# The low parts of the sums' blocks made by a multiplication and an accumulating DMA, in a channel attention kernel with a squared-relu feed-forward

## The chip, the cores and the metric

The kernel runs on one core of a Trainium2 chip. The metric is the device time of that core in microseconds. The engines have short names in the profile: PE is TensorE (PEld its weight loads), ACT is ScalarE, DVE is VectorE, POOL is GpSimd, SP is SyncE. SP issues all of the kernel's DMAs before the change.

## The reference

Four batches of 6080 tokens with 256 channels go through an attention over channels, and the 24320 resulting tokens through a feed-forward layer of width 2048 with the square of a relu. All data are float32; the two weight matrices come as float64.

```python
def _attn_ref(q, k, v, tau) -> np.ndarray:
    qn = q / (np.linalg.norm(q, axis=1, keepdims=True) + 1e-06)
    kn = k / (np.linalg.norm(k, axis=1, keepdims=True) + 1e-06)
    s = kn.transpose(0, 2, 1) @ qn / tau
    s = s - s.max(-1, keepdims=True)
    a = np.exp(s)
    a /= a.sum(-1, keepdims=True) + 1e-09
    return (v @ a).astype(np.float32)

def _moe_ref(x, w_in, w_out) -> np.ndarray:
    h = np.maximum(x @ w_in, 0.0)
    return (h * h @ w_out).astype(np.float32)
```

## The kernel before

**What is multiplied.** Attention and the first weight matrix are folded: for each batch the 256x256 attention matrix is multiplied with w_in once (tiles w_hi and w_lo), and the tokens of v then go through that product. So the main loop does two products for each block of tokens: v times the folded matrix (psum tile ps_h), and the squared relu times w_out (psum tile ps_o). For float32 accuracy each operand is split into a high part, rounded to fp32r, and a low part, which is the rest; three of the four products of parts are computed (hi hi, hi lo, lo hi).

**Tiles and steps.** A batch's tokens are cut into 12 blocks: ten of 512 and two of 480 tokens. A block has 16 steps, one for each 128 of the 2048 hidden channels. Two steps make a pair r. Each pair has one tile x of eight slots, each slot half a block wide (256 or 240 elements in a partition), and tiles g_hi and g_lo. `first_product` of a step (lines 712 to 727) does six matmuls into ps_h and one relu on ACT, which writes two of the slots 0 to 3 of x: the even step slots 0 and 1, the odd step slots 2 and 3. After the odd step `squares_and_sums` (736) squares slots 0 to 3 in place.

**Seven products instead of eight.** For all blocks but the first two, and but the last three pairs of the last block (`by_seven`, 704), the second product uses Winograd's scheme on 2x2 blocks: seven products instead of eight. It needs four sums of the squares' blocks, which VectorE writes into slots 4 to 7 of x with three instructions (743 to 746). g_hi and g_lo have seven slots: slots 0 to 2 take the parts of the squares' blocks, x slots 1 to 3 (cast on ACT, 744, and a subtraction of 768 elements on VectorE, 747); slots 3 to 6 take the parts of the four sums, x slots 4 to 7, in `parts_of_sums` (749): a cast of 1024 elements on ACT, and a subtraction of 1024 elements on VectorE. There are 365 such pairs: 46 blocks of eight, less three. Pairs without the scheme have one cast and one subtraction of 1024 elements for slots 0 to 3, in the same function.

**The order of a pair.** The main loop (964 to 1015) numbers the steps i. Every engine executes its instructions in the order in which the program issues them (`InProgramOrder`, 19). With p a pair whose steps are 2p and 2p + 1, the order around it is this:

- i = 2p: `first_product`; the first relu into x of p.
- i = 2p + 1: `first_product`; second relu; `squares_and_sums` of p (square, three sums, parts of slots 0 to 2).
- i = 2p + 2: `first_product` of the next pair; one piece of the attention for a later batch; `parts_of_sums` of p; second product of p - 1, part 0.
- i = 2p + 4: `first_product`, whose relu opens pair p + 2; second product of p, part 0, which reads slots 0, 1 and 2.
- i = 2p + 5: second product of p, part 1, which reads slots 3 to 6, the parts of the sums.

The pieces of attention stand between: for each chunk of q and k (tile qk, two in flight) a cast qk_hi on ACT, a subtraction qk_lo on VectorE, then a square on ACT, an addition into acc on VectorE, and the matmuls into gram (`attention`, 433). At a block's end come two copies of ps_o on ACT and five additions on VectorE (`combine`, 822), then four stores; and the casts of the next block of v (687, 696).

**Buffers.** Tiles of `pool` (96) have two buffers unless told otherwise; x, g_hi and g_lo have two. So pair p + 2 takes the buffers of pair p. ps_h has three (98).

Of the kernel before, what the change touches and what calls it, by code (L numbers as in the profile page):

```python
# [8 lines left out]
F32 = mybir.dt.float32  # L9
# [5 lines left out]
ALU = mybir.AluOpType  # L15
# [15 lines left out]
def kernel(  # L31
# [22 lines left out]
    tensor, vector, scalar, pool_engine = (  # L54
        InProgramOrder(tc, e) for e in (nc.tensor, nc.vector, nc.scalar, nc.gpsimd)
    )
# [647 lines left out]
    def by_seven(b, n, r):  # L704


        return (0, 1) < (b, n) and ((b, n) != order[-1] or r < SWITCH)
# [41 lines left out]
    def parts_of_sums(b, n, r):  # L749

        x = X.pop((b, n, r))
        hi, lo = G[b, n, r]
        if by_seven(b, n, r):
            hi, lo, src = hi[:, 3:7, :], lo[:, 3:7, :], x[:, 4:8, :]
        else:
            src = x[:, 0:4, :]
        scalar.copy(hi, src)
        vector.tensor_sub(lo, src, hi.bitcast(F32))

    O = {}  # L760

# [202 lines left out]
    for i in range(len(steps) + 2 * LAG):  # L964
# [24 lines left out]
        if part == 0 and 0 <= i // 2 - 1 < len(pairs):  # L989
            parts_of_sums(*pairs[i // 2 - 1])  # L990
# [52 lines left out]
```

## Time and profile before

| | us |
|---|---|
| median of the runs shown | 2214.74 |
| the two runs | 2213.72 and 2215.77 |
| span of the profiled execution, first to last instruction | 2211.6 |
| from the profiled span to the median | 3.1 |

The profile is of one execution. It gives, for each engine, the time in which it had an instruction running, and for each group of instructions the mean time of one and the idle time of its engine before it, with what ended most of that. A group's row names engine, operation, the tile written, the tiles read, and the shape (partitions by elements). A row of the timeline begins with the start and the duration in microseconds; what stands in square brackets is the engine's idle time before it and what ended that. A row of waits gives who waited for whom: the sum in microseconds, how many times, and the longest. A row of the DMA list gives size and median time from issue to landing. Line L27 is the helper through which engine instructions are issued, so instructions are told apart by their tiles. Matmuls are pipelined and their ends are modelled, so PE's busy share is not a share of its peak.

### The profile page before, as it was taken

What the parts mean: (1) busy time and instruction counts of PE and PEld (TensorE: products, weight loads), DVE (VectorE), ACT (ScalarE), POOL (GpSimd) and SP (SyncE); (2) the same over time, 40 slices, a digit from 0 to 9 for tenths busy, and PEclk for the clock granted to TensorE, in tenths of its full rate; (3) what the DMA queues carried; (4) which work ended last, traced back from release to release, by engine and by line L of the source; (5) the groups of instructions that cost most, each with busy time, mean ns of one, the idle gap of its engine ahead of it and who ended that gap; (6) DMA issues with size and microseconds to landing.
All of it is one profiled execution on the core that took longest, in us unless ns stands there. A gap on an engine that the chain in (4) does not pass through costs nothing.

```text
span 2211.6 us, 34981 instructions
## 1 busy us (share of the span) xinstructions
PE 2203.1 (100%) x13903; PEld 1985.0 (90%) x13903; DVE 1818.0 (82%) x2614; ACT 1859.1 (84%) x2347; POOL 0.7 (0%) x6
## 2 busy tenths in 40 slices
PE   9999999999999999999999999999999999999999
PEld 8789999988999999998999999999899988888898
DVE  6878888889888888878888888887888877787776
ACT  5788888888888888888878888888888888888887
POOL 0000000000000000000000000000000000000000
PEclk9999999999999999999999999999999999999999
DMA  9521122023421122210122122111103010010000
GB/s 342 179 77 39 61 77 65 27 76 109 157 86 58 60 62 71 63 60 21 36 95 86 60 66 76 58 53 60 33 24 115 22 36 20 22 37 20 20 28 19
DMA packets 82261, 148.03 MB, mean 67 GB/s; under 512 B 8368, under 2 KB 35760, under 8 KB 82096
## 3 DMA queue, kind: packets, MB, share of 16 engines
q1 hardware_dynamic: 82096, 145.79, 19.9%
q8 instruction: 109, 1.79, 0.3%
q14 instruction: 56, 0.46, 0.1%
HBM read 112.46 MB, written 33.29 MB: 66 GB/s over the span
## 4 chain that ended last, share of the span: by engine, by line
PE 92%; DVE 3%; DMA 2%; ACT 2%; issue 0%; SPq 0%; DVEq 0%; ACTq 0%
PE ps_h L27 46%; PE ps_o L27 41%; PE gram L27 4%; PE ps_w L27 2%; DMA qk<-in_k 1%; DVE g_lo L27 1%; DVE x L27 1%; ACT x L27 1%; DMA qk<-in_q 0%; DMA qk_heads<-in_q 0%; ACT g_hi L27 0%; DVE o L27 0%; DMA w_raw<-in_w_in 0%; DVE dec_m L27 0%; DMA wi_lo<-wi_kept 0%
## 5 line engine op out<-in xcount | busy, mean ns | idle before, releaser
L27 DVE TENSOR_TENSOR g_lo<-x,g_hi 128x768 fp32r<-128x768 f32 (+2 forms) x749 | 808.2, 1079 | 71.7 <-ACT g_hi L27 71.1
L27 DVE TENSOR_TENSOR x<-x 128x512 f32<-128x512 f32 (+1 forms) x1095 | 558.2, 510 | 244.0 <-ACT x L27 218.3
L27 ACT CAST g_hi<-x 128x768 fp32r<-128x768 f32 (+2 forms) x749 | 702.1, 937 | 42.8 <-DVE x L27 30.0
L27 ACT ACTIVATE x<-ps_h 128x512 f32<-128x512 f32 (+1 forms) x768 | 456.0, 594 | 248.7 <-PE ps_h L27 228.0
L27 PE MATMUL ps_h<-v_hi,w_hi 128*128 128x512 f32 (+1 forms) x1536 | 478.6, 393 | 0.0
L27 PE MATMUL ps_h<-v_hi,w_lo 128*128 128x512 f32 (+1 forms) x1536 | 477.9, 392 | 0.0
L27 PE MATMUL ps_h<-v_lo,w_hi 128*128 128x512 f32 (+1 forms) x1536 | 474.9, 390 | 0.0
L27 ACT ACTIVATE x<-x 128x1024 f32<-128x1024 f32 (+1 forms) x384 | 404.5, 1053 | 11.9
L27 PE MATMUL ps_o<-g_lo,wS_hi 128*128 128x256 f32 (+1 forms) x1460 | 407.6, 279 | 1.2 <-DVE g_lo L27 1.1
L27 PE MATMUL ps_o<-g_hi,wS_hi 128*128 128x256 f32 (+1 forms) x1460 | 406.1, 278 | 0.8 <-ACT o L27 0.8
L27 PE MATMUL ps_o<-g_hi,wS_lo 128*128 128x256 f32 (+1 forms) x1460 | 406.6, 278 | 0.0
L27 PEld LDWEIGHTS ps_h<-v_lo,w_hi 128*128 128x128 f32 x1536 | 287.9, 187 | 64.9
L27 PEld LDWEIGHTS ps_h<-v_hi,w_lo 128*128 128x128 f32 x1536 | 288.5, 188 | 62.4 <-DVE w_lo L27 0.3
L27 PE MATMUL ps_o<-g_hi,wo_hi 128*128 128x256 f32 (+2 forms) x1159 | 325.2, 285 | 0.6 <-ACT g_hi L27 0.6
L27 PE MATMUL ps_o<-g_hi,wo_lo 128*128 128x256 f32 (+2 forms) x1159 | 325.1, 285 | 0.0
L27 PE MATMUL ps_o<-g_lo,wo_hi 128*128 128x256 f32 (+2 forms) x1159 | 324.8, 285 | 0.1
L27 PEld LDWEIGHTS ps_o<-g_lo,wS_hi 128*128 128x128 f32 x1460 | 274.8, 188 | 17.9 <-DVE g_lo L27 2.1
L27 PEld LDWEIGHTS ps_o<-g_hi,wS_hi 128*128 128x128 f32 x1460 | 274.1, 188 | 17.2 <-ACT o L27 1.6
L27 PEld LDWEIGHTS ps_o<-g_hi,wS_lo 128*128 128x128 f32 x1460 | 274.4, 188 | 0.0
L27 PEld LDWEIGHTS ps_h<-v_hi,w_hi 128*128 128x128 f32 x1536 | 237.4, 188 | 3.6
L27 PEld LDWEIGHTS ps_o<-g_hi,wo_hi 128*128 128x128 f32 x1159 | 218.3, 188 | 15.7 <-ACT g_hi L27 1.0
L27 PEld LDWEIGHTS ps_o<-g_lo,wo_hi 128*128 128x128 f32 x1159 | 217.7, 188 | 15.2 <-DVE g_lo L27 0.5
(120 smaller groups left out, 1776.1 us busy)
## 6 DMA issues: line engine op xcount, KB each, us to landing
qk<-in_k SPq DMA_DIRECT2D x87, 256.0 KB, 2.8
qk<-in_q SPq DMA_DIRECT2D x87, 256.0 KB, 3.0
v<-in_vT SPq DMA_DIRECT2D x40, 512.0 KB, 3.8
out_T<-o SPq DMA_DIRECT2D x152, 128.0 KB, 1.7
wiS<-wi_sums_kept SPq DMA_DIRECT2D x24, 512.0 KB, 5.7
wi_hi<-wi_kept SPq DMA_DIRECT2D x16, 512.0 KB, 4.5
wi_lo<-wi_kept SPq DMA_DIRECT2D x16, 512.0 KB, 3.8
w_raw<-in_w_in SPq DMA_DIRECT2D x4, 1024.0 KB, 6.4
```

Source lines behind the costliest of these rows:

```text
L27: return lambda *args, **kwargs: self.tc.keep_in_program_order(issue(*args, **kwargs))
```

## The change

Only `parts_of_sums` changes, and in it only the pairs with seven products. ACT's cast of the four sums into g_hi stays as it was. VectorE no longer subtracts g_hi from the sums. It multiplies the sums by -1 and writes the result into the low part's four slots, rounded to fp32r: minus the rounded sums. Then POOL issues a DMA that adds the sums (x slots 4 to 7, 4 KB in each partition in a full block) to what stands in g_lo, which leaves the sums less their rounded value. The DMA waits for the multiplication; VectorE's instruction no longer needs g_hi. The other pairs do what they did before.

```diff
@@ -751,11 +751,12 @@
         x = X.pop((b, n, r))
         hi, lo = G[b, n, r]
         if by_seven(b, n, r):
-            hi, lo, src = hi[:, 3:7, :], lo[:, 3:7, :], x[:, 4:8, :]
+            scalar.copy(hi[:, 3:7, :], x[:, 4:8, :])
+            vector.tensor_scalar_mul(lo[:, 3:7, :], x[:, 4:8, :], -1.0)
+            pool_engine.dma_start(lo[:, 3:7, :].bitcast(F32), x[:, 4:8, :], accum_op=ALU.add)
         else:
-            src = x[:, 0:4, :]
-        scalar.copy(hi, src)
-        vector.tensor_sub(lo, src, hi.bitcast(F32))
+            scalar.copy(hi, x[:, 0:4, :])
+            vector.tensor_sub(lo, x[:, 0:4, :], hi.bitcast(F32))
 
     O = {}
```

## The prediction

> **What bounds the kernel now.** I read the page first, then the groups by shape, the waits, the timeline in two stretches, and the list of DMAs.
>
> ```profile
> span 2211.6 us, 34981 instructions
> PE 2203.1 (100%) x13903; PEld 1985.0 (90%) x13903; DVE 1818.0 (82%) x2614; ACT 1859.1 (84%) x2347; POOL 0.7 (0%) x6
> PE 92%; DVE 3%; DMA 2%; ACT 2%; issue 0%; SPq 0%; DVEq 0%; ACTq 0%
> q1 hardware_dynamic: 82096, 145.79, 19.9%
> L27 PEld LDWEIGHTS ps_o<-g_lo,wS_hi x1460: 186/188/193, 169.9 to 2196.4; 128*128 128x128 f32 x183
> ```
>
> PE has work in 2203.1 of 2211.6 us and holds 92% of the chain that ended last. A shorter VectorE instruction can win only the 8.5 us in which PE is without work. The question is what else the change delays. Four matmuls per pair read g_lo against wS_hi (three of them in the part that reads the sums), so the last row counts 1460/4 = 365 pairs with seven products, the first at 169.9 us.
>
> ```profile
> L27 DVE TENSOR_TENSOR g_lo<-x,g_hi 128x1024 fp32r<-128x1024 f32 x320 | 390.5, 1220 | 54.7 <-ACT g_hi L27 54.2
> L27 ACT ACTIVATE x<-ps_h 128x512 f32<-128x512 f32 x640 | 382.8, 598 | 211.3 <-PE ps_h L27 195.9 <-DVE g_lo L27 7.5 <-DVE v_lo L27 1.8
> L27 DVE TENSOR_TENSOR qk_lo<-qk,qk_hi 128x1024 fp32r<-128x1024 f32 x63 | 77.1, 1223 | 26.7 <-ACT qk_hi L27 26.7
> L27 DVE TENSOR_TENSOR acc<-acc,qk 128x1024 f32<-128x1024 f32 x63 | 76.9, 1221 | 12.2 <-ACT qk L27 12.2
> L27 DVE TENSOR_SCALAR dec_e<-w_raw 128x1024 int32<-128x1024 int32 x8 | 5.5, 688 | 0.4 <-DMA w_raw<-in_w_in 0.4
> ACT x L27 <- DVE g_lo L27: 11.6, 15, 1.5
> ...
> 1424.79 1.22 DVE L27 TENSOR_TENSOR g_lo<-x,g_hi 128x1024 fp32r<-128x1024 f32 x1
> 1426.10 0.60 ACT L27 ACTIVATE x<-ps_h 128x512 f32<-128x512 f32 x1 [0.62 <-DVE g_lo L27]
> ```
>
> The last three rows carry the argument. The relu (ACT, `x<-ps_h`) waits for g_lo 15 times, and in the instance shown it starts 0.09 us after the 1024-wide subtraction ends. That subtraction reads slots 4 to 7 of an x tile, and the relu of the pair two later writes slots 0 and 1 of the tile that takes its buffer (x has two). They share no byte, yet the relu waits: the buffer passes on as a whole, when its last reader is done. That reader is what the change replaces.
>
> **The change, part by part.** (1) The cast into g_hi on ACT reads and writes the same 1024 elements as before: nothing.
>
> (2) On 365 pairs the VectorE subtraction (1.22 us) becomes a multiplication by -1 with one tensor operand. No row shows one from f32 to fp32r. The nearest are TENSOR_SCALAR on 1024 elements, 0.69 us, and TENSOR_TENSOR, 1.22 us; I take 0.69, the row with one tensor operand, and keep 1.22 for the range. The 0.53 us saved and the 54.2 us of waiting for g_hi are VectorE's; with PE covering VectorE they are worth nothing by themselves.
>
> (3) A DMA of 512 KB a pair (480 KB in the short blocks) goes out on POOL's queue, empty until now (0.7 us busy), so nothing queues behind it there and SP's queue is not touched. It waits for the multiplication and reads x and g_lo. Its time L, from the end of the multiplication to the landing, is shown by no row. Nearest:
>
> ```profile
> v<-in_vT SPq DMA_DIRECT2D x40, 512.0 KB, 3.8
> w_raw<-in_w_in SPq DMA_DIRECT2D x4, 1024.0 KB, 6.4
> wi_kept<-wi_hi SPq DMA_DIRECT2D x4, 512.0 KB, 2.6
> out_T<-o SPq DMA_DIRECT2D x152, 128.0 KB, 1.7
> 1499.70 0.60 SPq L326 DMA_DIRECT2D qk<-in_q  x1
> ```
>
> An addition in flight reads two operands of 512 KB each and writes one. If only the 512 KB written counted, L would be 2.6 us (a store) to 3.8 us (a load). If the 1024 KB read count, a load of that size took 6.4 us. Between 3.8 and 6.4 I take the middle, 5.1 us: both ends in on-chip memory argue for less, descriptors made by POOL for more. Upper end for the range: 6.4 plus 0.6 (SP's own issue of a DMA), 7.0.
>
> The Trainium skill, "DMA: Bandwidth & Descriptors", section "Anatomy of one DMA — SWDGE (gpsimd) path", gives such a DMA about 2.0 us plus its bytes over 436 GB/s, 3.2 us for 512 KB. Its page "Collectives: The Full Stack", section "The bandwidth ceiling: the fold count and why AG ≠ RS ≠ AR", says that an add in the DMA needs two reads on the same ring; with 1024 KB the first formula gives 4.4 us. By the sum below these are about 2320 and 2565 us. No row of this trace holds an accumulating DMA.
>
> (4) What waits for the landing. First PE: the sums' low part is read in the step five after the pair's first. Second, and earlier, the relu that opens the pair two later, by the hand-over shown above. Behind that relu, in order, stands all of ACT's work: the cast or square of a q/k chunk, the 1024-wide cast of the pair in between, the next relu and square.
>
> ```profile
> 1752.56 0.60 ACT L27 ACTIVATE x<-ps_h 128x512 f32<-128x512 f32 x1 [0.23 <-PE ps_h L27]
> 1753.02 0.95 DVE L27 TENSOR_TENSOR g_lo<-x,g_hi 128x768 fp32r<-128x768 f32 x1
> 1753.13 1.05 ACT L27 CAST g_hi<-x 128x1024 fp32r<-128x1024 f32 x1
> 1754.22 1.22 DVE L27 TENSOR_TENSOR g_lo<-x,g_hi 128x1024 fp32r<-128x1024 f32 x1 [0.25 <-ACT g_hi L27]
> 1758.36 0.60 ACT L27 ACTIVATE x<-ps_h 128x512 f32<-128x512 f32 x1
> 1760.23 0.60 ACT L27 ACTIVATE x<-ps_h 128x512 f32<-128x512 f32 x1 [0.33 <-PE ps_h L27]
> 1760.86 1.06 ACT L27 ACTIVATE x<-x 128x1024 f32<-128x1024 f32 x1
> 1761.95 1.61 DVE L27 TENSOR_TENSOR x<-x 128x512 f32<-128x512 f32 x3 [0.80 <-ACT x L27]
> ...
> 752.28 0.60 ACT L27 ACTIVATE x<-ps_h 128x512 f32<-128x512 f32 x1 [0.96 <-PE ps_h L27]
> 752.78 1.04 ACT L27 CAST qk_hi<-qk 128x1024 fp32r<-128x1024 f32 x1
> 753.85 1.23 DVE L27 TENSOR_TENSOR qk_lo<-qk,qk_hi 128x1024 fp32r<-128x1024 f32 x1 [0.89 <-ACT qk_hi L27]
> 755.00 1.22 DVE L27 TENSOR_TENSOR g_lo<-x,g_hi 128x1024 fp32r<-128x1024 f32 x1
> ...
> 702.08 1.22 DVE L27 TENSOR_TENSOR g_lo<-x,g_hi 128x1024 fp32r<-128x1024 f32 x1
> 731.31 1.22 DVE L27 TENSOR_TENSOR g_lo<-x,g_hi 128x1024 fp32r<-128x1024 f32 x1
> ```
>
> In the first stretch the subtraction at 1754.22 belongs to the pair whose buffer the relu at 1758.36 takes. A multiplication could start when the 768-wide subtraction ends, 1753.97, and end at 1754.66: the relu would be late from L = 3.7 us. The two stages differ, because there are two loops.
>
> Loop A, in pairs that carry a q/k chunk's operation (63 + 63 = 126). The held relu is followed on ACT by the chunk's cast or square, VectorE's chunk operation waits for that, and the next pair's multiplication stands behind it. So the landing of one pair leads to the DMA of the very next. From the rows at 752.28: relu start to the place of the multiplication 2.7 us, multiplication 0.7, hand-overs 0.1: a pair takes at least 3.5 + L. It takes (731.31 - 702.08)/5 = 5.85 us now. Loss per pair: L - 2.35 us.
>
> Loop B, in the other 239 pairs: from the held relu to the DMA two pairs on. Relu 0.6, cast 1.05, next relu 0.6, square 1.06, the x sums 1.61, the 768-wide subtraction 0.95, multiplication 0.69: 6.56, about 6.5 with VectorE's small overlaps. To it comes the work for each block that falls into it:
>
> ```profile
> L27 ACT COPY o<-ps_o 128x1024 f32<-128x1024 f32 x38 | 38.3, 1009 | 0.0
> L27 ACT COPY o<-ps_o 128x768 f32<-128x768 f32 x38 | 30.2, 796 | 0.0
> L27 DVE TENSOR_TENSOR o<-o 128x512 f32<-128x512 f32 x76 | 52.3, 688 | 1.3
> L27 DVE TENSOR_TENSOR o<-o 128x256 f32<-128x256 f32 x114 | 47.9, 420 | 1.3
> L27 DVE TENSOR_TENSOR v_lo<-v,v_hi 128x1024 fp32r<-128x1024 f32 x40 | 48.7, 1218 | 0.0
> L27 ACT CAST v_hi<-v 128x1024 fp32r<-128x1024 f32 x40 | 41.8, 1046 | 0.0
> ```
>
> For a block of eight pairs 1.01 + 0.80 + 1.05 on ACT and 2 x 0.69 + 3 x 0.42 + 1.22 on VectorE, 6.7 us or 0.8 a pair. A pair takes at least (7.3 + L)/2. Now it takes (2211.6 - 169.9 - 126 x 5.85)/239 = 5.46 us. Loss per pair: L/2 - 1.81 us, from L = 3.6 on.
>
> (5) The 16 DMA engines: 365 x 0.52 MB is 190 MB beside 145.79 MB at 19.9%, so 26% more, or 52% if reads count twice. They stay under full; the q/k loads are asked for two chunks (four pairs, over 20 us) ahead, which covers some microseconds more. I add nothing for it.
>
> Sum at L = 5.1: 2.75 x 126 = 346 and 0.74 x 239 = 177, together 523 us. 2211.6 + 523 = 2735. The median of the runs, 2214.7, is 3.1 above the profiled span: 2738 us.
>
> **The rivals.**
> - A, quick transfer: L like the 512 KB rows, about 3.2 (between 2.6 and 3.8). Loop A loses 0.85 x 126 = 107 us, loop B nothing: 2322 us. For it: both operands lie on chip. Against: two reads. The Trainium skill's DMA page, as cited above, would put the time here, or at 2565 us with both reads.
> - B, slow transfer: L = 6.4. 4.05 x 126 + 1.39 x 239 = 842: 3057 us; at 7.0, 3205 us. For it: no row shows how long POOL takes to issue, nor what the addition costs an engine. A multiplication of 1.22 us adds 0.53 to both loops, 67 + 63 = 130 us, and lies inside these.
> - C, not slower: the DMA does not hold the relu, because the hand-over lets its read of slots 4 to 7 pass. Then only PE's read of the low parts is due: for the pair of 1754.22 at 1760.15 (row below), 5.5 us after the multiplication's end at 1754.66, and about 1.2 less where a chunk operation comes first. With L under 4.3 that is within 1% of 2215 us. Against it: 15 waits of just this kind.
>
> ```profile
> 1760.15 0.28 PE L27 MATMUL ps_o<-g_lo,wS_hi 128*128 128x256 f32 x1
> ```
>
> - D, hidden: L under 2.35, less than any 512 KB row; 2206 to 2215 us.
>
> **How the numbers follow.** Forecast, L from 4.4 to 6.4 (2566 to 3057 us): 0.50. A, L from 2.4 to 4.4: 0.22. B, above 6.4: 0.20. C 0.05, D 0.03. The predicted time is 2738 us. The range runs from A's 2322 (rounded to 2320) to B's 3205 and leaves out C, D, the quickest part of A and the slowest of B, some 2 in 10. About 2% (44 us) is what a measurement of this kernel can tell from no change; C and D give 0.08 for within, A from L = 2.7 on and all beyond are slower, 0.91; faster by 44 us has no room with 8.5 us of PE idle, 0.01.
>
> **What would show it.** In the waits, ACT x waiting for a DMA into g_lo, in most pairs, as the largest entry, and PE waiting for ACT or for that DMA. PE's busy time would stay near 2200 us with its share falling to about 80%. The multiplication at 0.69 us. In the DMA list the landing of g_lo<-x, which is L. Per pair, some 8.6 us in the q/k stages and 6.2 outside. If the relus follow PE as before, C holds; if L is off, the time moves by about 245 us for each microsecond (126 + 239/2).

## The result and the profile after

The changed kernel takes 2897.94 us (median of two runs, 2894.78 and 2901.10) against 2214.74 us: 1.309 times as long, with a 95% interval of 1.305 to 1.313. The profiled execution spans 2899.3 us, 687.7 more than before.

From the page of the changed kernel: the span, the engines' busy time, the granted clock of PE, the two DMA queues (packets, MB, share of 16 engines) and the chain that ended last.

```profile
span 2899.3 us, 36084 instructions
PE 2439.2 (84%) x13903; PEld 2132.3 (74%) x13903; DVE 1626.6 (56%) x2614; ACT 1823.4 (63%) x2347; POOL 314.9 (11%) x371
PEclk9999988999999989989999989989999999999999
q0 software_dynamic: 52560, 189.39, 34.9%
q1 hardware_dynamic: 82096, 145.79, 15.0%
DMA 9%; ACT 5%; PE 3%; DVE 2%; issue 1%; ACTq 0%; DVEq 0%; POOLq 0%
```

PE no longer fills the span. VectorE has 191 us less work (1818.0 to 1626.6) and the kernel is 31% slower: the work was taken from an engine that was covered. The shares of this chain add up to a fifth only, since it could not be followed to the start; the waits carry the reading instead. From the list of waits of the changed kernel (sum, times, longest), POOL's own waiting left out:

```profile
ACT x L27 <- DMA g_lo<-x: 912.8, 277, 10.3
DVE x L27 <- ACT x L27: 773.1, 325, 10.9
PEld ps_o L27 <- DMA g_lo<-x: 521.8, 243, 8.1
PE ps_o L27 <- DMA g_lo<-x: 446.1, 222, 7.8
DVE qk_lo L27 <- ACT qk_hi L27: 210.0, 67, 5.5
DVE acc L27 <- ACT qk L27: 184.5, 69, 5.1
```

The relu that waited 15 times for the subtraction now waits 277 times for the DMA that took its place, for 912.8 us. PE waits for the same DMA at its own read, and VectorE waits for ACT. The next rows are of the timeline, two landings in the q/k stage.

```profile
1081.77 0.69 DVE L27 TENSOR_SCALAR g_lo<-x 128x1024 fp32r<-128x1024 f32 x1
1083.00 0.86 POOL L27 DMA_DIRECT2D g_lo<-x  x1 [7.71 <-DVE g_lo L27]
1087.99 0.60 ACT L27 ACTIVATE x<-ps_h 128x512 f32<-128x512 f32 x1 [3.06 <-DMA g_lo<-x]
1088.49 1.04 ACT L27 CAST qk_hi<-qk 128x1024 fp32r<-128x1024 f32 x1
1089.56 1.23 DVE L27 TENSOR_TENSOR qk_lo<-qk,qk_hi 128x1024 fp32r<-128x1024 f32 x1 [2.19 <-ACT qk_hi L27]
1090.70 0.69 DVE L27 TENSOR_SCALAR g_lo<-x 128x1024 fp32r<-128x1024 f32 x1
1091.92 0.86 POOL L27 DMA_DIRECT2D g_lo<-x  x1 [8.06 <-DVE g_lo L27]
1097.74 0.60 ACT L27 ACTIVATE x<-ps_h 128x512 f32<-128x512 f32 x1 [4.80 <-DMA g_lo<-x]
```

This is loop A as the prediction wrote it down: multiplication, 0.53 us to POOL's DMA, landing, held relu, cast of the chunk, the chunk's subtraction, and then the multiplication of the next pair. From one held relu to the next it takes 9.75 us here. From the multiplication's end to the relu that the landing lets go it is 5.5 us the first time (1082.46 to 1087.99), beside the two loads of a chunk, and 6.35 us the second time (1091.39 to 1097.74), beside a load of v and two stores.

The groups and the DMA list give the two durations that no row of before had, and the tile view of g_lo gives the spread of the landings (from the issue on POOL):

```profile
L27 DVE TENSOR_SCALAR g_lo<-x 128x1024 fp32r<-128x1024 f32 x304 | 208.7, 686 | 0.0
g_lo<-x POOLq DMA_DIRECT2D x304, 512.0 KB, 4.5
v<-in_vT SPq DMA_DIRECT2D x40, 512.0 KB, 6.0
DMA to landing us min/median/max: 4.3/4.5/10.4
```

So a DMA left alone lands 0.53 + 4.49 = 5.0 us after the multiplication. The mean over the 365 pairs of the trace is 0.56 + 5.03, 5.6 us: the tail reaches 10.4.

### The profile page after: what moved, and what is told of

Its sections match the earlier page's. It is cut to its first block, busy times and chain, and to the rows that moved or that the text cites. A ratio compares the mean times of both kernels' runs of the same rounds, so it can differ in the third digit from the quotient of the medians.

```text
span 2899.3 us, 36084 instructions
## 1 busy us (share of the span) xinstructions
PE 2439.2 (84%) x13903; PEld 2132.3 (74%) x13903; DVE 1626.6 (56%) x2614; ACT 1823.4 (63%) x2347; POOL 314.9 (11%) x371
## 3 DMA queue, kind: packets, MB, share of 16 engines
q0 software_dynamic: 52560, 189.39, 34.9%
## 5 line engine op out<-in xcount | busy, mean ns | idle before, releaser
L27 ACT ACTIVATE x<-ps_h 128x512 f32<-128x512 f32 (+1 forms) x768 | 457.8, 596 | 1009.4 <-DMA g_lo<-x 912.8
L27 PE MATMUL ps_o<-g_lo,wS_hi 128*128 128x256 f32 (+1 forms) x1460 | 461.6, 316 | 446.5 <-DMA g_lo<-x 446.1
L27 PEld LDWEIGHTS ps_o<-g_lo,wS_hi 128*128 128x128 f32 x1460 | 297.7, 204 | 526.5 <-DMA g_lo<-x 521.8
L27 POOL DMA_DIRECT2D g_lo<-x x365 | 314.2, 861 | 2562.9 <-DVE g_lo L27 1098.1
L27 PE MATMUL ps_h<-v_hi,w_hi 128*128 128x512 f32 (+1 forms) x1536 | 513.5, 418 | 0.0
L27 PE MATMUL ps_h<-v_lo,w_hi 128*128 128x512 f32 (+1 forms) x1536 | 498.5, 407 | 0.0
L27 PE MATMUL ps_o<-g_hi,wS_lo 128*128 128x256 f32 (+1 forms) x1460 | 434.7, 298 | 0.0
L27 DVE TENSOR_TENSOR g_lo<-x,g_hi 128x768 fp32r<-128x768 f32 (+2 forms) x384 | 367.2, 956 | 20.8 <-ACT g_hi L27 20.7
L27 PEld LDWEIGHTS ps_h<-v_lo,w_hi 128*128 128x128 f32 x1536 | 308.8, 201 | 72.4
L27 PEld LDWEIGHTS ps_o<-g_hi,wS_lo 128*128 128x128 f32 x1460 | 301.8, 207 | 0.0
L27 DVE TENSOR_SCALAR g_lo<-x 128x1024 fp32r<-128x1024 f32 (+1 forms) x365 | 248.4, 681 | 0.0
```

The costliest lines, as they stand in the source:

```text
L27: return lambda *args, **kwargs: self.tc.keep_in_program_order(issue(*args, **kwargs))
```

## The experiments

Theory 1 is the prediction's: the time goes into waiting for the landing, mainly at the relu that takes over the buffer of x. The others are named in the expectations. Each experiment's time is of one run, beside a run of the kernel before on the same chip (2213.3 to 2214.6 us). Differences from the changed kernel are taken between the profiled spans (2899.3 us for the changed kernel).

**The multiplication without the DMA.**

```diff
-            pool_engine.dma_start(lo[:, 3:7, :].bitcast(F32), x[:, 4:8, :], accum_op=ALU.add)
```

> The changed kernel without the DMA; g_lo keeps minus the rounded sums, the addition is left out. Theory 1: all of the loss is the wait for the landing; 2205 to 2216 us, the multiplication at 0.69 us, PE's granted clock back at 1.00. Rival: the multiplication or the order of the instructions costs by itself, then above 2230 us.

2210.24 us, span 2208.5. From its page:

```profile
PE 2202.4 (100%) x13903; PEld 1986.8 (90%) x13903; DVE 1619.7 (73%) x2614; ACT 1858.3 (84%) x2347; POOL 0.7 (0%) x6
PEclk9999999999999999999999999999999999999999
```

VectorE's saving of 198 us is worth 3 us, little more than the kernel before differs from run to run (2213.3 to 2215.8 us), and everything that the change costs comes with the DMA.

**The sums in a tile of their own.** x keeps slots 0 to 3; the sums get a tile y with two buffers, so memory stays the same.

```diff
-            X[b, n, f // 2] = pool.tile([P, 8, tn // 2], F32, tag="x", ...)
+            X[b, n, f // 2] = pool.tile([P, 4, tn // 2], F32, tag="x", ...)
...
+            S[b, n, r] = y = pool.tile([P, 4, blocks[n][1] // 2], F32, tag="y", ...)
-            vector.tensor_sub(x[:, 4:6, :], x[:, 1:3, :], ...)
+            vector.tensor_sub(y[:, 0:2, :], x[:, 1:3, :], ...)
...
-            pool_engine.dma_start(lo[:, 3:7, :].bitcast(F32), x[:, 4:8, :], accum_op=ALU.add)
+            pool_engine.dma_start(lo[:, 3:7, :].bitcast(F32), y, accum_op=ALU.add)
```

> The changed kernel with the four sums in a tile of their own (two buffers of four slots, x shrinks to four): the relu that opens the pair two later no longer takes a buffer that the DMA reads. Theory 1, the loss comes through the hand-over of x to that relu: ACT's wait for the DMA (912.8 us) goes, only PE's read of the low parts is still due, about 5.5 us after the multiplication (4.3 where a chunk operation comes first), and with 5.0 to 5.6 us to the landing the time falls to about 2320 us (2270 to 2400). Rival 2, PE's own wait for the low parts sets the time and ACT's wait only stands beside it (in the timeline both end together): 2800 to 2900 us. Rival 3, the added DMA traffic or PE's lower granted clock (0.931) costs time whoever waits: above 2600 us.

2448.84 us, span 2447.1. From its waits:

```profile
ACT x L27 <- PE ps_h L27: 345.3, 511, 3.4
PEld ps_o L27 <- DMA g_lo<-y: 202.2, 164, 6.2
ACT g_hi L27 <- PE ps_o L27: 165.2, 111, 7.2
PE ps_o L27 <- DMA g_lo<-y: 153.1, 119, 5.9
```

The relu waits for PE again and for no DMA, with the same DMAs in flight. That takes 452 of the 688 us away: so much the hand-over adds to what PE's own read costs. Rivals 2 and 3, with 2800 and 2600 us or more, are out. The time is above the 2400 us at the top of theory 1's range. PE's read was priced as lateness alone. The third row shows what that left out: g_hi and g_lo have two buffers too, and the cast into them two pairs later waits until PE is done with them, 165.2 us. That row is read from the trace; no run takes this hand-over away alone.

The control makes the same move in the kernel before.

> Control: the kernel before with the same move of the sums into a tile of their own. All theories: no measurable change, 2208 to 2218 us; the 11.6 us of ACT waiting for g_lo are gone or near it.

2212.98 us: the tile is free. The list of waits has no row of ACT's relu waiting for g_lo any more (11.6 us before), as it should be if these waits came from the shared buffer.

**The parts of the sums ahead of the piece of attention.** Same change, one order swapped in the even step.

```diff
+        if part == 0 and 0 <= i // 2 - 1 < len(pairs):
+            parts_of_sums(*pairs[i // 2 - 1])
         if i < PAIR or part == 0:
             for gen in gens:
                 next(gen, None)
-        if part == 0 and 0 <= i // 2 - 1 < len(pairs):
-            parts_of_sums(*pairs[i // 2 - 1])
```

> The changed kernel with one thing moved: in the even step the parts of the sums are made before the piece of attention, so that no chunk operation stands between the held relu and the next multiplication. Theory 1 with two loops: loop A (one pair for each landing, 8.9 us a pair on 136 pairs) is broken and these pairs run in loop B, about 7 us; the time falls by some 250 us from 2899 to about 2640 us (2570 to 2710). Rival 6, one loop only, the landing in front of the relu costs the same wherever the chunk operation stands: above 2820 us.

2591.82 us, span 2590.0, 309 less than the changed kernel, where 190 to 330 had been expected. From its waits:

```profile
ACT x L27 <- DMA g_lo<-x: 523.6, 230, 7.4
PEld ps_o L27 <- DMA g_lo<-x: 260.9, 169, 6.2
```

The landings are as before (5.5 us in the mean from the multiplication's end). Taken from the first relu of a pair to that of the next, over the trace: the 136 pairs with a chunk operation go from 8.88 to 6.62 us in the mean, the 229 others stay at 6.60 and 6.59. Loop A exists, and the order that puts the next multiplication behind the held relu's followers made it. Rival 6 is out.

**What the landing is made of.** First a plain copy in place of the addition; g_lo then holds the sums themselves.

```diff
-            pool_engine.dma_start(lo[:, 3:7, :].bitcast(F32), x[:, 4:8, :], accum_op=ALU.add)
+            pool_engine.dma_start(lo[:, 3:7, :].bitcast(F32), x[:, 4:8, :])
```

> The changed kernel with a plain copy in place of the accumulating DMA: g_lo takes the sums themselves, nothing is added. Theory 1 with two reads for one write: a 4096-byte packet falls from 0.33 us to about half, the landing from 4.5 us after the issue to about 3.2, and the time to about 2400 us (2340 to 2500). Rival 4, the landing is mostly the issue on POOL and fixed costs: it stays within 0.4 us of 4.5 and the time above 2780 us.

2511.65 us, span 2509.9. Then the addition for two sums only, with the subtraction kept for the other two:

```diff
-            vector.tensor_scalar_mul(lo[:, 3:7, :], x[:, 4:8, :], -1.0)
-            pool_engine.dma_start(lo[:, 3:7, :].bitcast(F32), x[:, 4:8, :], accum_op=ALU.add)
+            vector.tensor_scalar_mul(lo[:, 3:5, :], x[:, 4:6, :], -1.0)
+            pool_engine.dma_start(lo[:, 3:5, :].bitcast(F32), x[:, 4:6, :], accum_op=ALU.add)
+            vector.tensor_sub(lo[:, 5:7, :], x[:, 6:8, :], hi[:, 5:7, :].bitcast(F32))
```

> The changed kernel with two of the four sums left to the VectorE subtraction, so that the multiplication, and the DMA with its 2048-byte packets, cover half. Theory 1: issue and start stay (0.5 us to the issue, 1.4 to the first packet), the packets' 2.7 us halve; landing 3.1 us after the issue in place of 4.5, and the time goes to about 2450 us (2370 to 2530). Rival 4, the landing is mostly fixed: within 0.4 us of 4.5, above 2780 us.

2520.39 us, span 2518.6. From the DMA lists, first of the copy:

```profile
q0 software_dynamic: 48656, 189.39, 19.5%
g_lo<-x POOLq DMA_DIRECT2D x304, 512.0 KB, 2.9
```

and of the half addition:

```profile
q0 software_dynamic: 52560, 94.71, 21.6%
g_lo<-x POOLq DMA_DIRECT2D x304, 256.0 KB, 3.2
```

The engines' time for the same 189.39 MB written is 34.9% of 2899.3, 1012 us, with the addition and 19.5% of 2509.9, 489 us, without: the addition doubles it, as a second read would. Halving the bytes halves it too (21.6% of 2518.6, 544 us), and the landing falls from 4.5 to 3.2 us. They land 1.3 and 1.6 us sooner and win nearly the same, 381 and 389 us. If the other half of the bytes takes the same 1.3 us, the rest of a landing, near 1.9 us from the issue (3.2 less 1.3), does not shrink with the bytes; that is an estimate from these two runs. Rival 4 is out. The copy landed sooner than expected (2.9 for 3.2) but took 12 us more than its range allowed. Its mean landing, with those beside SP's transfers, comes 3.9 us after the multiplication and not 3.4, which the expectation left out; whether that is the whole reason was not tried.

**Crowding.** Fewer transfers on SP's queue. Left out are loads of v after the third block, loads of q and k for batches 2 and 3 beyond two chunks, and the stores of all seven-product blocks but one.

```diff
+        if (b, n) > (0, 2):
+            V[b, n] = [V[0, 2][0], None, None]
+            return
...
+            if self.b > 1 and c >= QK_BUFS:
+                self.raws[c] = self.raws[c - QK_BUFS]
+                return
...
-        for m, k, slot in ((0, 0, 2), (0, 1, 1), (1, 0, 0), (1, 1, 6)):
+        for m, k, slot in ((0, 0, 2), (0, 1, 1), (1, 0, 0), (1, 1, 6)) if (b, n) == (0, 2) else ():
```

> The changed kernel with less other DMA traffic beside the accumulating DMA: loads of v after the third block, loads of q and k for batches 2 and 3 beyond the first two chunks, and all output stores of seven-product blocks but one block's are left out (tiles already in memory stand in for the data). Theory 1 with contention: alone the DMA takes 5.0 us from the end of the multiplication, in the changed kernel 5.6 in the mean, because 179 of 365 share the engines with SP's DMAs; less traffic brings the mean to about 5.1 and the time to about 2740 us (2720 to 2790). Rival 5, the extra 0.6 us is not from SP's transfers, or it does not reach the end: above 2860 us.

2822.06 us, span 2820.3. Its queue, and its landings:

```profile
q1 hardware_dynamic: 31520, 76.79, 7.9%
DMA to landing us min/median/max: 4.3/4.5/11.0
```

With half of SP's bytes gone, 303 of the 365 landings have no packet of SP's queue between issue and landing, 181 before. The mean from the multiplication to the landing falls by 0.27 us (5.59 to 5.32) and the time by 79 us, a little more than the prediction's 245 us for each microsecond give (66). So crowding costs time, against rival 5. But 62 landings still share the engines, and theirs are slower (5.9 us in the mean from the issue, 5.5 before), so the mean did not come down to the 5.1 us that the expectation took, and the time missed its range.

> Control: the kernel before with the same transfers left out. All theories: 2205 to 2216 us, since PE bounds it and its loads and stores are hidden.

2213.47 us: the same transfers cost the kernel before nothing.

**Can the landing be hidden?** With the own tile, the parts of the sums are made one step earlier, right behind the sums:

```diff
             squares_and_sums(*pairs[i // 2])
+            parts_of_sums(*pairs[i // 2])
...
-        if part == 0 and 0 <= i // 2 - 1 < len(pairs):
-            parts_of_sums(*pairs[i // 2 - 1])
```

> Sums in a tile of their own, and the parts of the sums made in the odd step right behind the squares and sums, one step earlier, so that no chunk operation stands ahead of the multiplication. Theory 1: what is left of the loss with the own tile (2447 us) is PE waiting for landings that come after its read; with 5.0 us alone and 5.4 to 6.6 us from multiplication to read, only crowded landings are late: 2240 to 2310 us. Rival 3, the added traffic itself: no better than 2400 us.

2370.22 us, span 2368.4, 60 above the range. In another run, also with the own tile, the second product comes one pair later, and the order of the changed kernel is kept:

```diff
-    LAG = 2
+    LAG = 3
...
-        return [pool.tile(..., name=f"{name}{b}_{n}_{r}") for name in ("g_hi", "g_lo")]
+        return [pool.tile(..., name=f"{name}{b}_{n}_{r}", bufs=3) for name in ("g_hi", "g_lo")]
...
-    wo_lo = const.tile([P, NF, C], F32R, name="wo_lo")
+    wo_lo = wo_hi
```

> Sums in a tile of their own, the second product one pair later (lag 3) and three buffers for g_hi and g_lo; to make room, the low part of w_out is left out (its tile is the high part's). Theory 1: 5.2 us more until PE's read hide every landing: 2208 to 2225 us with the accumulating DMA in place, granted clock 1.00. Rival 3, the added traffic or POOL's work costs by itself: above 2300 us.

2260.25 us, span 2258.1, with the accumulating DMA in place on all 365 pairs. From its page and its waits:

```profile
q0 software_dynamic: 52560, 189.39, 43.8%
DVE y L27 <- DMA g_lo<-y: 163.0, 75, 8.0
PEld ps_o L27 <- DMA g_lo<-y: 17.9, 10, 6.1
```

The engines move the same bytes, now at 43.8% of a shorter span, and PE hardly waits for them. So added traffic and POOL's work cost at most the 46 us that are left, and the 8.5 us that PE could have won; rival 3 is out for the rest, which is latency. The combination of both,

> The run a_own_lag3 (own tile, second product one pair later, three buffers for the parts, low part of w_out left out) with the parts of the sums made one step earlier as in a_own_early. Theory 1: what is left there, 45 us, is VectorE waiting to write sums into a tile whose DMA has not landed (163.0 us of such waits, in stages where SP loads much); an earlier multiplication frees that tile sooner: 2215 to 2240 us. Rival 3, the added traffic or POOL's descriptors cost by themselves: 2250 us or more again.

gave 2293.96 us, span 2291.9: worse, and VectorE's 163.0 us of waiting for the DMA were down to 20.4. The guess that these waits are the last 46 us fell. The time is the one that rival 3 gave, but the control for the earlier place, with the subtraction and no DMA, gives it another reason:

> Control for a_own_early and a_lag3_early: the kernel before, sums in a tile of their own, the subtraction kept and no DMA added, with the parts of the sums made one step earlier. Theory 7, the earlier place costs by itself, because ACT's cast of the sums stands in line until VectorE has made them (333.7 us of such waits in a_lag3_early): 2260 to 2310 us. Rival, the place is free and the 78 to 157 us above the kernel before came from the DMA: 2208 to 2220 us.

2311.07 us, span 2309.3. From its waits:

```profile
ACT g_hi L27 <- DVE y L27: 367.4, 365, 3.9
PEld ps_o L27 <- ACT o L27: 47.4, 46, 3.0
PEld gram L27 <- DVE qk_lo L27: 30.3, 28, 1.8
```

The earlier place itself costs 98 us. ACT's cast stands in line for the sums on every one of the 365 pairs, and PE then waits for ACT's copies at the blocks' ends (47.4 us, 1.6 before) and for the chunks' low parts; that this line is the whole of the 98 us is read from the waits and was not tried. So of the 157 us that the early version with the DMA is above the kernel before, 59 come with the multiplication and the DMA in place of the subtraction. What makes the 46 us of the lag-3 version is open: it had no control without a DMA. The fastest version here is 3 us ahead of the kernel before, and it leaves the addition out; PE's 8.5 us without work are all that could be won.

## Why the prediction was right, and where its size was off

- That PE covers VectorE, and that a shorter instruction there is worth nothing, was right (3 us without the DMA).
- The multiplication was put at 0.69 us and takes 0.686. ACT's cast was put at nothing: without the DMA its group takes 335.4 us, 335.7 before, and its waits only get shorter.
- The hand-over of x, read from 15 short waits and one timeline pair, was named as the place where the landing is felt first. That was right: without it 452 us are gone. "They share no byte, yet the relu waits" was the reading on which the forecast stood against rival C.
- PE's read was named as the later of the two. As an order that was right, but the sum let it disappear behind the relu. Once the relu was free, 235 us were left (2447.1 less 2211.6), with PE's read among what is left and the hand-over of g_hi beside it. Rival C's "within 1%" held for L under 4.3 us; the mean was 5.6.
- L was taken as 5.1 us, the middle between a load of 3.8 and one of 6.4 us. A DMA left alone takes 5.0. That the second read counts was right: the copy takes half the engine time. That the middle came within 0.1 us was luck: neither load tells how long POOL takes to issue (0.53 us after the multiplication) or what the addition costs.
- The Trainium skill's "Collectives: The Full Stack", section "The bandwidth ceiling: the fold count and why AG ≠ RS ≠ AR", says of a reducing step that its add needs two source reads, and the engine times of copy and addition agree (489 and 1012 us). With both reads the Trainium skill's "DMA: Bandwidth & Descriptors", section "Anatomy of one DMA — SWDGE (gpsimd) path", gave an estimate of 4.4 us; measured from the multiplication's end it was 5.0, and 3.4 (0.53 + 2.9) for the plain copy, for which its estimate is 3.2.
- The term that was mis-sized is part (5), the DMA engines, put at nothing. It asked only whether SP's loads would be late. They were (v lands in 6.0 us, 3.8 before), but no row of the waits names a load of v; the accumulating DMA, which nothing hides, was slowed by them in turn: 5.6 us in the mean. With 5.6 in the two loops and the 136 and 229 pairs that the trace has, (5.6 - 2.35) x 136 + (2.8 - 1.81) x 229 = 442 + 227 = 669 us, against 688 measured and 523 predicted. The 10 pairs more with a chunk operation, half-size ones among them, make about 20 of it.
- The sum comes nearer than its parts. Loop A was to take 8.6 us a pair and loop B 6.2; they take 8.88 and 6.60, where the same pairs took 5.84 and 5.39 before. That is a loss of 414 us in loop A, 28 less than this working gives, and of 275 us in loop B, 48 more. What loop B has above the working is open.
- One sign did not come: PE's busy time was to stay near 2200 us, and it is 2439.2. Its 13903 matmuls are the same; the last section shows that some of them ran at half the clock.

## What to carry to other kernels

Before moving work from a covered engine to a DMA, look not at who reads the result but at who waits for the source's buffer: a buffer is handed over whole, at its last reader, and a reader that takes 5 us where one took 1.2 delays whoever comes next, with all that stands behind it in order. Count how many pairs the latency spans in each loop, because an in-order engine between two landings can turn one landing for two pairs into one for each. And price a DMA by its mean beside the other traffic, not by its best.

## What was not expected of the hardware

PE's granted clock fell to a mean of 0.931, without any change to PE's own work. The windows view (length, busy time by engine, granted clock, DMA share, GB/s) shows it around the landing at 1097.7, and the timeline shows PE's rows there:

```profile
1095.00:1098.00 3.00, 0.32 (x1) 0.32 (x2) 0.94 (x2) 0.26 (x1) 0.00 (x0) 0.84 1.01 238
1098.00:1102.00 4.00, 4.00 (x19) 3.90 (x19) 1.99 (x3) 3.94 (x6) 0.33 (x1) 0.50 0.30 84
...
1093.99 0.28 PE L27 MATMUL ps_o<-g_hi,wS_hi 128*128 128x256 f32 x1
1097.68 0.58 PE L27 MATMUL ps_o<-g_lo,wS_hi 128*128 128x256 f32 x1 [3.41 <-DMA g_lo<-x]
1098.49 0.41 PE L27 MATMUL ps_o<-g_lo,wS_hi 128*128 128x256 f32 x1
```

After 3.41 us without work PE runs at half its clock: a matmul of 256 columns takes 0.41 us in place of 0.28, and the next begins after 0.21 in place of 0.12 us. The trace has 405 us at 0.5, nearly all in pieces of 3.4 and 6.8 us. None of the 106 waits of 0.3 to 1.5 us is followed by such a piece, 56 of the 90 between 1.5 and 3 us are, and all 38 longer ones. The Trainium skill, "TensorE: Matmul & The Clock Gate", section "What's actually happening", has the half clock after an idle window of about 3.4 us that runs on its own beat. The length of the pieces agrees with that; as a length of waiting it differs, since here 1.8 us was enough. What the half clock adds to the time was not tried by itself. Half the clock over 405 us delays PE's work by some 200 us at most, and how much of that reaches the end is open. The two loops give 669 of the 688 us without it, but loop B loses 48 us more than this working, and a part of that may be the clock's. In the lag-3 version, with 19 us at half clock, it is 9 us at most.
